# Attention and the first FFN's beginning emitted from an explicit list of pieces instead of a loop

## The chip, the cores and the metric

The kernel runs on one core of a Trainium2 chip. What counts is the device time in microseconds (us) of one execution. The kernel before took 602.12 us (median of 3 runs, 602.09 to 603.09). The execution that the profiler recorded took 603.07 us; its span, from the first to the last instruction, is 601.3 us.

## The reference

Band-and-summary attention over 2 batches, 8 heads, 768 positions and a head width of 64, and then two feed-forward networks (FFNs) over the 1536 resulting rows of 512, with 2048 inner columns each. All is float32.

```python
# attention: a query sees keys less than 16 positions away, and one summary per block of 32 keys
k_sum = k.reshape(B, H, nb, 32, D).max(axis=3)      # nb = 24 summaries
v_sum = v.reshape(B, H, nb, 32, D).mean(axis=3)
scores_l = where(|i - j| < 16, scale * q @ k.T, -1e9)
scores_s = scale * q @ k_sum.T + log(32)
a = softmax(concat([scores_l, scores_s]))            # denominator + 1e-9
x = a @ concat([v, v_sum])                           # then heads side by side: 1536 x 512
# first FFN, second FFN
h = x @ w_in;  g = h - tanh(h);              x = g @ w_out
h = x @ w_in2; g = h * tanh(log1p(exp(h)));  out = g @ w_out2
```

## The kernel before, in words

**Attention** is cut into 12 units of 128 query positions over all 8 heads (UPB = 6 units for each batch). A unit u passes through these steps, each on a fixed engine; `e` is one of two halves of the heads:

- `qk(u)`, PE: 32 score products into the PSUM tiles s (e = 0) and tr (e = 1), two buffers each (L300 to L314). It needs the queries (tile qt, three buffers), the unit's keys with their edges (tile kt, eight buffers), and the key summaries of the whole batch, which `k_sum` (DVE, one block maximum for each unit) makes and `k_fill` copies to both ends of kt. So the first unit of a batch waits for the keys of all six.
- `softmax(u, e)`: four DVE instructions add the mask and find the maximum (aa, neg), four ACT instructions take the exponential and its sum (L316 to L332).
- `norm(u)`: a reciprocal on DVE, and the multiplication of each half on POOL or DVE (L334 to L344).
- `a_trans(u, e)`: four PE transposes into the PSUM tile aT, and a copy to asb on DVE or ACT (L346 to L356).
- `av(u)`: 32 PE products with the values and value summaries (tile vu, three buffers) into the PSUM tile x (L363). The value summaries are sums by DVE or POOL (`v_sum`), a transpose, two ACT copies and four small copies within the chip (`v_trans`, `v_fill`).
- `x_hi(u)`, ACT, and `x_lo(u)`, DVE: the result as a rounded high part and the rest, the FFN's input.

**The FFNs** go over three chunks c of 512 rows, and within one over 16 steps i of 128 inner columns. A step is `ffn_in` (12 products of 128x512 on PE into s or aT), the gate (ACT tanh, DVE subtraction, ACT `g_hi`, DVE `g_lo`), and `ffn_out` (12 products, accumulated over i in x, x, tr, tr). The products are taken three times: high by high, high by low, low by high.

**The weights** come as float64 bits and are converted in 64 pieces of 256 columns for each FFN. A piece n is loaded (`conv_load`, SP), and passes `conv_top` (ACT), `conv_or` (DVE), `conv_hi` (ACT or POOL) and `conv_lo` (DVE or POOL). Six pieces can be in flight between load and `conv_or` (n_raw = 6). The first chunk's steps use each weight for the first time, so there conversion runs beside the products; later chunks use what is there.

**What sets the order.** The scheduler is off (`tc.manual_schedule`, L615): every engine carries out its instructions in the order in which the code emits them, and so does the queue of SP, which issues all DMAs and stops at one whose buffer isn't free yet. Attention's order comes from the loop over half-units j (L439 to L471): for every j it emits the scores of unit j/2, the softmax of half j-1, the normalization and the transpose of half j-5, the values of unit (j-6)/2, and what a table `todo` puts at this j (loads, block sums, fills). From j = 19 on the tables AHEAD and AFTER say how many conversion steps (`conv_tick`) go in, HI_POOL and LO_POOL whether on POOL; the first FFN's steps 0 to 5 start at fixed j through `more_in`. Then the FFN loop (L621) goes on, from n = 0, with four conversion steps for each n.

Of the kernel before, what the change touches and what calls it, by code (L numbers as in the profile page):

```python
# [26 lines left out]
def kernel(  # L27
# [17 lines left out]
    nc = tc.nc  # L45
# [125 lines left out]
    ASB_DVE = (0, 2, 7, 11, 12, 13, 14, 15, 17, 20, 21)  # L171
    NORM_DVE = (0, 13, 21, 23)
    FILL_DVE = (0, 1, 4, 5, 6, 7, 8, 9, 11)
    AHEAD = {23: 1, 24: 3, 29: 3, 31: 1}
    AFTER = {19: 1, 21: 1, 22: 1, 25: 1, 28: 3, 30: 1}
    HI_POOL = (19, 21, 22, 24, 25, 30)
    LO_POOL = (19, 22, 23, 24, 25, 28, 29, 30, 31)

    def attention(actx):
# [80 lines left out]
        def k_fill(u):  # L260
            eng = nc.vector if u in FILL_DVE else nc.gpsimd
            for o in (0, NB + KU):
                eng.tensor_copy(kt[u % NK][:, :, o:o + NB], ksum[u // UPB])

        def v_sum(b, g, part, pool=False):
            if b not in vsum:
                vsum[b] = two.tile([128, HP, NB], F32, tag="vsum", name="vsum")
            t = vtc[b, g].rearrange("p a (n c) -> p a n c", c=BLK)
            o = vsum[b][:, :, g * 8:(g + 1) * 8]
            t, o = (z[:, 2 * part:2 * part + 2] for z in (t, o))  # L270
            if not pool:
# [20 lines left out]
        def v_fill(n):  # L292
# [5 lines left out]
        sums, neg, aa, asb, xps, sc = {}, {}, {}, {}, {}, {}  # L298
# [17 lines left out]
        def softmax(u, e):  # L316
            w, pv = u % UPB, sc.pop((u, e))
            if e == 0:
                aa[u] = two.tile([128, 2, HP, KA], F32, tag="aa", name="aa", bufs=3)
                neg[u] = two.tile([128, 2, HP], F32, tag="neg", name="neg", bufs=3)  # L320
                sums[u] = two.tile([128, 2, HP], F32, tag="sums", name="sums", bufs=3)
            m = masks[0 if w == 0 else 2 if w == UPB - 1 else 1]
            for hp in range(HP):
                nc.vector.tensor_tensor_reduce(  # L324
                    out=aa[u][:, e, hp, :], in0=pv[:, hp, :], in1=m, scale=-1.0 / math.sqrt(D),
                    scalar=3.0e38, op0=ALU.add, op1=ALU.min, accum_out=neg[u][:, e, hp:hp + 1],
                )
            for hp in range(HP):
                nc.scalar.activation(  # L329
                    out=aa[u][:, e, hp, :], in_=aa[u][:, e, hp, :], func=ACTF.Exp,  # L330
                    scale=-1.0, bias=neg[u][:, e, hp:hp + 1], accum_out=sums[u][:, e, hp:hp + 1],
                )  # L332

        def norm(u):  # L334
            r = two.tile([128, 2, 2, HP], F32, tag="rd", name="rd")
# [4 lines left out]
            for e in range(2):  # L340
                (nc.vector if 2 * u + e in NORM_DVE else nc.gpsimd).tensor_tensor(
                    out=aa[u][:, e], in0=aa[u][:, e],
                    in1=r[:, 1, e, :].unsqueeze(2).to_broadcast([128, HP, KA]), op=ALU.mult,
                )  # L344
# [77 lines left out]
        at(11, L(load_vt, 1, 2), L(v_sum, 1, 0, 0))
        at(12, L(v_sum, 1, 0, 1, True), L(conv_ahead, n_raw))
        at(13, L(v_sum, 1, 1, 0))
        at(14, L(v_sum, 1, 1, 1, True))
        at(15, L(v_sum, 1, 2, 0, True))
        at(16, L(v_sum, 1, 2, 1))
        before_av[17] = L(v_trans, 1)
        at(17, L(v_fill, 1), L(v_fill, 2))
        for u in range(7, 12):  # L430
            at(2 * u - 3, L(k_fill, u))
        NJ = 2 * NU
        LT, LA = 5, 6

        def ticks(j, counts):
            for _ in range(counts.get(j, 0)):
                conv_tick(len(pieces) // 2, j in HI_POOL, j in LO_POOL)

        for j in range(NJ + LA + 2):  # L439
            if j in (NJ, NJ + 1, NJ + 5):  # L440
                more_in(n_in)
            if j == NJ:
                kq_x.close()
                more_w(4)
            xu, xr = divmod(j - LA - 2, 2)
            if xu >= 0 and not xr:
                x_hi(xu)
            if j < NJ and j % 2 == 0:
                qk(j // 2)
            nu, nr = divmod(j - 3, 2)  # L450
            nr = nr == 0 and 0 <= nu < NU
            if 1 <= j <= NJ:
                softmax(*divmod(j - 1, 2))
            ticks(j, AHEAD)
            if nr:
                norm(nu)
            if xu >= 0 and xr:
                x_lo(xu)
            if LT <= j < NJ + LT:
                a_trans(*divmod(j - LT, 2))  # L460
            if j in before_av:
                before_av[j]()
            if LA <= j < NJ + LA and (j - LA) % 2:
                av((j - LA) // 2)
# [40 lines left out]
    def gate_1(z):  # L505
        h = hs.pop(z)
        t = ts[z] = tmp.tile([128, CH], F32, tag="t", name="t")
        nc.scalar.activation(out=t, in_=h, func=ACTF.Tanh)
        nc.vector.tensor_tensor(out=t, in0=h, in1=t, op=ALU.subtract)

    def gate_1s(z):
        g_hi(z, ts[z])
        g_lo(z, ts.pop(z))
# [101 lines left out]
    with tc.manual_schedule():  # L615
        with ExitStack() as actx:
            attention(actx)
        more_w(NI - len(W))
        N2 = NC * NI
        limit = len(pieces) // 2  # L620
        for n in range(NS + 2):  # L621
# [17 lines left out]
            if f == 0:  # L639
# [14 lines left out]
                if n and n + 1 < N2:  # L654
                    gate_1(steps[n + 1])
# [102 lines left out]
```

## Time and profile before

| | |
|---|---|
| median of 3 runs | 602.12 us (602.09 to 603.09) |
| the profiled execution | 603.07 us, span 601.3 us |
| PE busy over the span | 578.8 us (96%) |
| DVE, ACT, POOL busy | 417.8, 328.5, 53.4 us |
| last unit's value products (av of unit 11) start | 82.01 us |
| bytes moved by DMA | 52.20 MB |

One execution is profiled; its instructions have a start and a duration, and an idle engine's next instruction names what released it. The profile's stretches are counted from the span's start. PE's busy time is 60.33 us in the first 79 us and has no gap behind that for hundreds of us, so the first 79 us are the stretch to look at: attention, with the first FFN's beginning in its last third.

### The profile page before, as it was taken

What the parts mean: (1) busy time and instruction counts of PE and PEld (TensorE: products, weight loads), DVE (VectorE), ACT (ScalarE), POOL (GpSimd) and SP (SyncE); (2) the same over time, 40 slices, a digit from 0 to 9 for tenths busy, and PEclk for the clock granted to TensorE, in tenths of its full rate; (3) what the DMA queues carried; (4) which work ended last, traced back from release to release, by engine and by line L of the source; (5) the groups of instructions that cost most, each with busy time, mean ns of one, the idle gap of its engine ahead of it and who ended that gap; (6) DMA issues with size and microseconds to landing.
All of it is one profiled execution on the core that took longest, in us unless ns stands there. A gap on an engine that the chain in (4) does not pass through costs nothing.

```text
span 601.3 us, 9203 instructions
## 1 busy us (share of the span) xinstructions
PE 578.8 (96%) x3212; PEld 479.0 (80%) x3212; DVE 417.8 (69%) x968; ACT 328.5 (55%) x791; POOL 53.4 (9%) x109
## 2 busy tenths in 40 slices
PE   6768899999999999999999999999999999999997
PEld 5556788888888888888888888888888888888885
DVE  5797978886251222377776489997688777597785
ACT  4788878885251122367765456664464444454442
POOL 6465660000000000000000000000000000000000
PEclk9798899999999999999999999999999999999999
DMA  9997567765020000226661102100100000100001
GB/s 271 257 306 213 154 184 238 222 218 168 0 88 0 1 0 1 62 88 192 197 186 43 40 8 63 52 2 1 55 16 1 1 1 0 71 1 1 1 1 70
DMA packets 32110, 52.20 MB, mean 87 GB/s; under 512 B 3200, under 2 KB 25728, under 8 KB 32064
## 3 DMA queue, kind: packets, MB, share of 16 engines
q1 hardware_dynamic: 32064, 51.62, 28.5%
q8 instruction: 25, 0.41, 0.3%
q14 instruction: 21, 0.17, 0.1%
HBM read 48.07 MB, written 3.15 MB: 85 GB/s over the span
## 4 chain that ended last, share of the span: by engine, by line
PE 88%; DMA 4%; DVE 3%; ACT 2%; SPq 1%; issue 1%; POOL 0%; ACTq 0%
PE aT L478 7%; PE aT L479 7%; PE tr L479 7%; PE x L479 7%; PE aT L480 7%; PE tr L480 7%; PE x L480 7%; PE x L478 7%; PE tr L478 7%; PE s L479 7%; PE s L478 7%; PE s L480 7%; DMA kt<-in_kw_dram 3%; ACT aa L329 1%; DMA vtc<-in_vt_dram 1%; PE x L363 1%
## 5 line engine op out<-in xcount | busy, mean ns | idle before, releaser
L503 DVE TENSOR_TENSOR glo<-t,ghi 128x512 fp32r<-128x512 f32 x48 | 33.4, 695 | 85.4 <-ACT ghi L498 85.4
L498 ACT ACTIVATE ghi<-t 128x512 fp32r<-128x512 f32 x48 | 30.2, 629 | 96.5 <-PE tr L480 96.5
L478 PE MATMUL aT<-xhi,w 128*128 128x512 f32 x192 | 74.9, 390 | 0.0
L478 PE MATMUL s<-xhi,w 128*128 128x512 f32 x192 | 74.9, 390 | 0.0
L480 PE MATMUL s<-xhi,w 128*128 128x512 f32 x192 | 74.7, 389 | 0.0
L480 PE MATMUL aT<-xhi,w 128*128 128x512 f32 x192 | 74.7, 389 | 0.0
L479 PE MATMUL s<-xlo,w 128*128 128x512 f32 x192 | 74.7, 389 | 0.0
L479 PE MATMUL aT<-xlo,w 128*128 128x512 f32 x192 | 74.7, 389 | 0.0
L114 ACT ACTIVATE top<-raw 128x256 f16<-128x256 bf16 x128 | 61.5, 486 | 12.2 <-ACT w L132 4.8
L121 DVE SCALAR_TENSOR_TENSOR cv<-raw,top 128x256 int32<-128x256 int32 x128 | 55.4, 434 | 11.8 <-ACT top L114 7.6
L132 ACT ACTIVATE w<-cv 128x256 fp32r<-128x256 f32 x120 | 47.6, 402 | 10.7 <-DVE cv L121 9.8
L137 DVE TENSOR_TENSOR w<-cv,w 128x256 fp32r<-128x256 f32 x114 | 48.4, 426 | 0.1
L534 DVE SCALAR_TENSOR_TENSOR t<-n,r 128x512 f32<-128x512 f32 x48 | 33.1, 689 | 17.4 <-ACT r L531 17.3
L503 DVE TENSOR_TENSOR glo<-n,ghi 128x512 fp32r<-128x512 f32 x48 | 33.1, 690 | 15.5 <-ACT ghi L498 15.5
L498 ACT ACTIVATE ghi<-n 128x512 fp32r<-128x512 f32 x48 | 30.3, 632 | 24.4 <-PE tr L479 16.1
L329 ACT ACTIVATE aa<-aa,neg 128x120 f32<-128x120 f32 x96 | 36.6, 384 | 12.4 <-DVE neg L324 12.4
L480 PEld LDWEIGHTS aT<-xhi,w 128*128 128x128 f32 x192 | 36.1, 188 | 7.5
L480 PEld LDWEIGHTS s<-xhi,w 128*128 128x128 f32 x192 | 36.1, 188 | 7.5
L478 PEld LDWEIGHTS aT<-xhi,w 128*128 128x128 f32 x192 | 36.0, 188 | 7.5
L478 PEld LDWEIGHTS s<-xhi,w 128*128 128x128 f32 x192 | 36.0, 188 | 7.5
L479 PEld LDWEIGHTS s<-xlo,w 128*128 128x128 f32 x192 | 36.0, 188 | 7.4
L479 PEld LDWEIGHTS aT<-xlo,w 128*128 128x128 f32 x192 | 36.0, 188 | 7.4
(97 smaller groups left out, 1293.1 us busy)
## 6 DMA issues: line engine op xcount, KB each, us to landing
raw<-in_w_dram SPq DMA_DIRECT2D x128, 255.8 KB, 3.6
vu<-in_vw_dram SPq DMA_DIRECT2D x24, 192.0 KB, 4.9
qt<-in_qt_dram SPq DMA_DIRECT2D x12, 256.0 KB, 4.9
vtc<-in_vt_dram SPq DMA_DIRECT2D x6, 512.0 KB, 6.7
out_dram<-o SPq DMA_DIRECT2D x9, 256.0 KB, 2.0
kt<-in_kw_dram SPq DMA_DIRECT2D x6, 320.0 KB, 8.5
kt<-in_kw_dram SPq DMA_DIRECT2D x6, 256.0 KB
out_dram<-t SPq DMA_DIRECT2D x3, 256.0 KB
```

The source lines that it names most:

```text
L114: nc.scalar.activation(out=tops[n % len(tops)].bitcast(F16).rearrange("p (n t) -> p n t", t=2)[:, :, 1], in_=raws[n].bitcast(BF16).rearran ...
L121: nc.vector.scalar_tensor_tensor(out=tmps[n], in0=raws.pop(n).bitcast(I32).rearrange("p (n t) -> p n t", t=2)[:, :, 0], scalar=13, in1=top ...
L132: nc.scalar.activation(out=hi, in_=t, func=ACTF.Copy)
L137: (nc.gpsimd if on_pool else nc.vector).tensor_tensor(out=W[i][:, 1, o:o + PW], in0=tmps.pop(n).bitcast(F32), in1=W[i][:, 0, o:o + PW].bit ...
L329: nc.scalar.activation(out=aa[u][:, e, hp, :], in_=aa[u][:, e, hp, :], func=ACTF.Exp, scale=-1.0, bias=neg[u][:, e, hp:hp + 1], accum_out= ...
L363: nc.tensor.matmul(out=xps[u][64 * e:64 * e + 64, hp, T * s:T * s + T], lhsT=vu[u % 3][:, s, 2 * hp + e, :], rhs=asb[u, e][:, hp, T * s:T ...
L478: nc.tensor.matmul(out=out, lhsT=w[0], rhs=x[0], start=first, stop=False)
L479: nc.tensor.matmul(out=out, lhsT=w[0], rhs=x[1], start=False, stop=False)
L480: nc.tensor.matmul(out=out, lhsT=w[1], rhs=x[0], start=False, stop=last)
L498: nc.scalar.activation(out=ghi, in_=t, func=ACTF.Copy)
L503: nc.vector.tensor_tensor(out=glo, in0=t, in1=ghi.bitcast(F32), op=ALU.subtract)
L534: nc.vector.scalar_tensor_tensor(out=ts[z], in0=ns[z], scalar=2.0, in1=rs[z], op0=ALU.add, op1=ALU.mult)
```

## The change

The loop over j, its tables and `todo` go. In their place stands one string of 463 names (the change's title counts 500), read from left to right; each name is a step with its unit, half or piece, and a star where a step can run on two engines. `mx` and `ex` are the two halves of what was `softmax`, `rd` and `nm` those of `norm`, `tr` and `as` the transposes and their copy, `ct`, `co`, `ch` and `cw` the four conversion steps, `in` and `ou` the FFN's products, `th`, `sb`, `gh` and `gl` the gate, and `ld...`, `cl` the loads. A star puts `kf`, `nm` and `as` on DVE, and `vs`, `ch` and `cw` on POOL. The tiles aa and neg are now one for each half instead of one for both. The list goes as far as the product `in5` and 33 pieces of conversion; the FFN loop then starts at n = 4 instead of 0.

```diff
-    ASB_DVE = (0, 2, 7, 11, 12, 13, 14, 15, 17, 20, 21)
-    NORM_DVE = (0, 13, 21, 23)
-    FILL_DVE = (0, 1, 4, 5, 6, 7, 8, 9, 11)
-    AHEAD = {23: 1, 24: 3, 29: 3, 31: 1}
-    AFTER = {19: 1, 21: 1, 22: 1, 25: 1, 28: 3, 30: 1}
-    HI_POOL = (19, 21, 22, 24, 25, 30)
-    LO_POOL = (19, 22, 23, 24, 25, 28, 29, 30, 31)
+    SEQ = """
+    ldk5 ldk4 ks5 ks4 ldk2 ks2 ldk0 ks0 ldk1 ks1 ldk3 ks3 kf4* kf2* ke4 ke3 ke1 ke2 ke5 kf0 ldq0 qk0
+    mx0.0 ex0.0 kf1 ldt0.0 mx0.1 ex0.1 vs0.0.0 vs0.0.1* kf3 ldq1 qk1 mx1.0 mx1.1 ex1.1 ex1.0 rd0
...
+    ldv11 cl14 as11.1 av11 cl15 cl16 in3 cl17 gh1 ct13 ct14 co13 co14 ch12* cw12* gl0 xh11 xl11 ct15
...
+    """.split()
...
-        def softmax(u, e):
+        def max_(u, e):
             w, pv = u % UPB, sc.pop((u, e))
-            if e == 0:
-                aa[u] = two.tile([128, 2, HP, KA], F32, tag="aa", name="aa", bufs=3)
-                neg[u] = two.tile([128, 2, HP], F32, tag="neg", name="neg", bufs=3)
-                sums[u] = two.tile([128, 2, HP], F32, tag="sums", name="sums", bufs=3)
+            aa[u, e] = two.tile([128, HP, KA], F32, tag=f"aa{e}", name="aa", bufs=3)
+            neg[u, e] = two.tile([128, HP], F32, tag=f"neg{e}", name="neg", bufs=3)
...
-        for j in range(NJ + LA + 2):
-            if j in (NJ, NJ + 1, NJ + 5):
-                more_in(n_in)
-            if j == NJ:
+        starred = ("kf", "vs", "nm", "as", "ch", "cw")
+        for z in SEQ:
+            f = z.rstrip("0123456789.*")
+            do[f](*(int(n) for n in z[len(f):].rstrip("*").split(".")), *([z[-1] == "*"] if f in starred else []))
+            if z == f"qk{NU - 1}":
                 kq_x.close()
                 more_w(4)
...
+            if z == f"av{NU - 1}":
+                actx.close()
+                more_w(NI - len(W))
...
-        for n in range(NS + 2):
+        for n in range(n_in - 2, NS + 2):
```

SP's queue, in the middle of attention's first batch: kt_95, kt_96 and kt_89 to kt_92 are the buffers that take the second batch's six key loads, vu the values, qt the queries, and a row `vu_101<-vu_100` is the copy of the value summaries. Before:

```order
L244 DMA vu_101<-in_vw_dram 96x512 x2
L240 DMA qt_97<-in_qt_dram 128x512
L244 DMA vu_102<-in_vw_dram 96x512 x2
L221 DMA kt_95<-in_kw_dram 128x4x160
L221 DMA kt_96<-in_kw_dram 128x4x160
L240 DMA qt_98<-in_qt_dram 128x512
L221 DMA kt_89<-in_kw_dram 128x4x160
L240 DMA qt_99<-in_qt_dram 128x512
L294 DMA vu_101<-vu_100 24x512 x2
L294 DMA vu_102<-vu_100 24x512 x2
L221 DMA kt_90<-in_kw_dram 128x4x160
L221 DMA kt_91<-in_kw_dram 128x4x160
```

And now:

```order
L270 DMA vtc<-in_vt_dram 128x1024
L243 DMA kt_96<-in_kw_dram 128x4x160
L243 DMA kt_89<-in_kw_dram 128x4x160
L262 DMA qt_98<-in_qt_dram 128x512
L243 DMA kt_90<-in_kw_dram 128x4x160
L266 DMA vu_100<-in_vw_dram 96x512 x2
L243 DMA kt_91<-in_kw_dram 128x4x160
L243 DMA kt_92<-in_kw_dram 128x4x160
L262 DMA qt_99<-in_qt_dram 128x512
L319 DMA vu_101<-vu_100 24x512 x2
L266 DMA vu_101<-in_vw_dram 96x512 x2
L243 DMA kt_95<-in_kw_dram 128x4x160
```

Five of the six key loads now stand ahead of the value summaries' copies, and one, kt_95, behind the first of them and a pair of value loads; before, three stood ahead and three behind.

POOL's queue, where the first conversion steps (w<-cv) stand among the normalizations (aa<-aa,rd). Before:

```order
L341 TENSOR_TENSOR aa<-aa,rd 128x480 x2
L263 COPY kt_91<-ksum 128x4x24 x2
L341 TENSOR_TENSOR aa<-aa,rd 128x480 x2
L130 CAST w_73<-cv 128x256
L341 TENSOR_TENSOR aa<-aa,rd 128x480 x2
L130 CAST w_73<-cv 128x256
```

And now:

```order
L285 COPY kt_94<-ksum 128x4x24 x2
L370 TENSOR_TENSOR aa<-aa,rd 128x480 x2
L285 COPY kt_95<-ksum 128x4x24 x2
L370 TENSOR_TENSOR aa<-aa,rd 128x480 x2
L285 COPY kt_89<-ksum 128x4x24 x2
L285 COPY kt_90<-ksum 128x4x24 x2
L370 TENSOR_TENSOR aa<-aa,rd 128x480 x2
L130 CAST w_73<-cv 128x256
```

Most fills (kt<-ksum) have come over from DVE to POOL: 9 of 12, against 3 before.

PE's queue around the last three units' value products (x<-asb), with their transposes (aT<-ident,aa) and one FFN product (aT<-xhi,w). Before:

```order
L349 MATMUL aT<-ident,aa 120x128 x4
L363 MATMUL x<-asb,vu_100 64x64 x16
L349 MATMUL aT<-ident,aa 120x128 x8
L363 MATMUL x<-asb,vu_101 64x64 x16
L349 MATMUL aT<-ident,aa 120x128 x4
L478 MATMUL aT<-xhi_67,w_75 128x512
```

And now:

```order
L378 MATMUL aT<-ident,aa 120x128 x8
L394 MATMUL x<-asb,vu_102 64x64 x16
L378 MATMUL aT<-ident,aa 120x128 x8
L394 MATMUL x<-asb,vu_100 64x64 x16
L378 MATMUL aT<-ident,aa 120x128 x8
L394 MATMUL x<-asb,vu_101 64x64 x16
L441 MATMUL aT<-xhi_67,w_75 128x512
```

The third FFN product stands between the values of units 10 and 11 in both; the first two have moved forward, to between the scores of units 9 and 10 and behind those of unit 11, and each unit's second transpose stands ahead of the value products of the unit before.

## Rows read from the trace of the kernel before

**Rows 1.** Stretches of the span: length, busy time by engine, clock, DMA share, GB/s.
```profile
core 0: us, PE busy (x) PEld busy (x) DVE busy (x) ACT busy (x) POOL busy (x), PEclk, DMA share, GB/s
0.00:82.00 82.00, 63.33 (x912) 52.25 (x912) 64.00 (x292) 61.76 (x249) 47.89 (x101) 0.90 0.81 232
11.50:82.00 70.50, 56.02 (x844) 45.33 (x844) 58.48 (x276) 58.39 (x238) 41.19 (x67) 0.88 0.80 229
97.00:145.00 48.00, 48.00 (x213) 39.75 (x213) 40.21 (x100) 38.80 (x99) 0.00 (x0) 1.00 0.71 219
```

**Rows 2.** PE in order of time, last value products: start, length, instructions.
```profile
82.01 1.15 PE L363 MATMUL x<-asb,vu 120*64 120x64 f32 x32
...
96.83 0.39 PE L478 MATMUL aT<-xhi,w 128*128 128x512 f32 x1
```

**Rows 3.** DVE's waits from 11.5 to 82 us: total, times, longest.
```profile
DVE ksum L255 <- DMA kt<-in_kw_dram: 4.9, 3, 2.9
DVE asb L353 <- PE aT L349: 2.9, 2, 1.6
DVE cv L121 <- ACT top L114: 1.3, 2, 1.1
DVE aa L324 <- PE tr L310: 1.0, 1, 1.0
```

**Rows 4.** ACT's longest wait, same stretch.
```profile
ACT aa L329 <- DVE neg L324: 12.4, 12, 2.6
```

**Rows 5.** DVE's groups up to 82 us: count, then busy us, mean ns.
```profile
L353 DVE COPY asb<-aT 120x512 f32<-120x512 f32 x11 | 7.4, 674 | 2.9 <-PE aT L349 2.9
L375 DVE TENSOR_TENSOR xlo<-x,xhi 128x512 fp32r<-128x512 f32 x10 | 6.6, 656 | 0.0
L121 DVE SCALAR_TENSOR_TENSOR cv<-raw,top 128x256 int32<-128x256 int32 x11 | 5.8, 533 | 2.2 <-ACT top L114 1.3 <-issue 0.8
L263 DVE COPY kt<-ksum 128x96 f32<-128x96 f32 x18 | 5.8, 377 | 0.1
L341 DVE TENSOR_TENSOR aa<-aa,rd 128x480 f32<-128x480 f32 x4 | 3.0, 753 | 0.1
```

**Rows 6.** ACT's groups up to 82 us.
```profile
L355 ACT ACTIVATE asb<-aT 120x512 f32<-120x512 f32 x13 | 7.5, 581 | 0.3 <-PE aT L349 0.3
L114 ACT ACTIVATE top<-raw 128x256 f16<-128x256 bf16 x12 | 5.5, 485 | 0.2 <-DVE cv L121 0.2
L132 ACT ACTIVATE w<-cv 128x256 fp32r<-128x256 f32 x4 | 1.6, 404 | 0.1
```

**Rows 7.** The chain of waits before unit 6's scores: start, length, what.
```profile
14.94 8.57 DMA kt<-in_kw_dram
...
30.19 4.37 DMA kt<-in_kw_dram
...
34.58 0.70 DVE ksum L255
```

**Rows 8.** SP's queue in order of time: the value summaries' copies, then key loads.
```profile
21.30 3.32 SPq L294 DMA_DIRECT2D vu<-vu  x4
24.84 1.76 SPq L221 DMA_DIRECT2D kt<-in_kw_dram  x2
```

**Rows 9.** PE in order of time: unit 6's first score product.
```profile
36.13 0.31 PE L310 MATMUL s<-kt,qt 64*64 64x120 f32 x1
```

**Rows 10.** POOL and DVE near 64 us, and the same DVE instruction later.
```profile
63.35 2.11 POOL L341 TENSOR_TENSOR aa<-aa,rd 128x480 f32<-128x480 f32 x2 [2.25 <-PE x L363]
...
64.54 1.20 DVE L137 TENSOR_TENSOR w<-cv,w 128x256 fp32r<-128x256 f32 x1
...
L137 DVE TENSOR_TENSOR w<-cv,w x26: 417/419/422, 90.0 to 119.9; 128x256 fp32r<-128x256 f32 x26
```

**Rows 11.** POOL's groups up to 82 us.
```profile
L341 POOL TENSOR_TENSOR aa<-aa,rd 128x480 f32<-128x480 f32 x20 | 20.8, 1055 | 22.8 <-DVE rd L339 10.1 <-ACT aa L329 6.5 <-PE x L363 5.9
L263 POOL COPY kt<-ksum 128x96 f32<-128x96 f32 x6 | 1.4, 265 | 0.0
```

More of the change, by code (lines that the diff above doesn't have):

```diff
@@ new lines @@
+    sb0 co3 ch3* co4 qk10 mx10.1 mx10.0 ex9.0 rd9 cl5 ct5 ldq11 cl6 cl7 vf1.1 av6 xh6 xl6 tr8.0
+    ex10.1 ex10.0 kf11 qk11 ct6 co5 mx11.1 ct7 ex11.1 as8.0* cw3* in1 ldv7 av7 xh7 nm9.0* tr9.0
+    as9.0 as8.1* rd10 nm9.1* mx11.0 ch4* cw4* xl7 tr9.1 as9.1* co6 co7 ex11.0 rd11 vf1.2 ldv8 av8
+    xh8 xl8 nm10.0 nm10.1 tr10.1 as10.1 ch5* tr10.0 as10.0* cl8 ct8 co8 gh0 ch6 ldv9 av9 cw5* cw6
+    ch7* ch8 cw7 cw8 xh9 xl9 cl9 ct9 co9 cl10 ldv10 ct10 co10 nm11.0 tr11.0 as11.0 th1 sb1 nm11.1
+    tr11.1 av10 in2 xh10 xl10 cl11 ct11 co11 cl12 cl13 ct12 co12 ch9* ch10* cw9 ch11* cw10 cw11
@@ new lines @@
+    ldv11 cl14 as11.1 av11 cl15 cl16 in3 cl17 gh1 ct13 ct14 co13 co14 ch12* cw12* gl0 xh11 xl11 ct15
+    ct16 cl18 cl19 cl20 ch13* cw13 ch14 gl1 co15 ct17 ch15 co16 cw14 cw15 ch16* cw16* cl21 cl22 co17
+    cl23 ch17 ct18 ct19 co18 cl24 ct20 ch18* co19 cl25 ct21 th2 cw17 co20 cw18* co21 ch19* cw19 ct22
+    sb2 co22 ct23 co23 cl26 cl27 cl28 ch20 ch21* cw20 cw21* ct24 th3 ct25 ch22 cw22 co24 ct26 co25
+    ct27 cl29 cl30 ou0 ou1 ch23 ch24 cw23 co26 co27 ct28 gh2 ct29 sb3 gl2 ch25 ch26 co28 cw24* co29
@@ L179, in attention @@
+    cw25 ct30 co30 cl31 cl32 ct31 cw26 co31 ch27 cw27* ch28* ch29* cw28 cw29* ct32 ch30* cw30* cl33
+    cl34 cl35 cl36 cl37 in4 th4 ch31 sb4 gh3 gl3 in5
+    """.split()
     def attention(actx):
@@ L339, in norm, with a_out @@
             nc.vector.reciprocal(out=r[:, 1], in_=r[:, 0])
[L340 to L344, printed above, removed]
+        def norm(u, e, star):
+            r = sums[u, 1]
+            (nc.vector if star else nc.gpsimd).tensor_tensor(
+                out=aa[u, e], in0=aa[u, e],
+                in1=r[:, 1, e, :].unsqueeze(2).to_broadcast([128, HP, KA]), op=ALU.mult,
+            )
         def a_trans(u, e):
-            p = pst("aT")
+            p = at[u, e] = pst("aT")
             for hp in range(HP):
-                nc.tensor.transpose(p[0:KA, hp * 128:(hp + 1) * 128], aa[u][:, e, hp, :], ident)
+                nc.tensor.transpose(p[0:KA, hp * 128:(hp + 1) * 128], aa[u, e][:, hp, :], ident)
+        def a_out(u, e, star):
             t = two.tile([KA, HP, 128], F32, tag=f"asb{e}", name="asb")
-            pv = p[0:KA, :].rearrange("p (a n) -> p a n", a=HP)
-            if 2 * u + e in ASB_DVE:
+            pv = at.pop((u, e))[0:KA, :].rearrange("p (a n) -> p a n", a=HP)
+            if star:
                 nc.vector.tensor_copy(t, pv)
@@ L422, in attention @@
[L422 to L437, printed above, removed]
@@ L439, in attention @@
-        for j in range(NJ + LA + 2):
-            if j in (NJ, NJ + 1, NJ + 5):
-                more_in(n_in)
-            if j == NJ:
+        do = dict(
+            ldk=lambda u: (load_k_own if u < UPB else load_k)(u), ldq=load_q, ldv=load_v, ldt=load_vt,
+            ks=k_sum, ke=k_edges, kf=k_fill, vs=v_sum, vt=v_trans, vE=v_out, vf=v_fill,
+            qk=qk, mx=max_, ex=exps, rd=recip, nm=norm, tr=a_trans, av=av, xh=x_hi, xl=x_lo,
+            cl=conv_load, ct=conv_top, co=conv_or, ch=conv_hi, cw=conv_lo,
+            th=lambda i: gate_1t(steps[i]), sb=lambda i: gate_1m(steps[i]),
+            gh=lambda i: g_hi(steps[i], ts[steps[i]]), gl=lambda i: g_lo(steps[i], ts.pop(steps[i])),
+            ou=more_out,
+        )
@@ L443, in attention @@
+        do["as"] = a_out
+        do["in"] = more_in
+        starred = ("kf", "vs", "nm", "as", "ch", "cw")
[3 more added lines that the diff above has]
+            if z == f"qk{NU - 1}":
                 kq_x.close()
                 more_w(4)
[L445 to L464, printed above, removed]
@@ L503, in g_lo, with gate_1t, gate_1m @@
         nc.vector.tensor_tensor(out=glo, in0=t, in1=ghi.bitcast(F32), op=ALU.subtract)
-    def gate_1(z):
-        h = hs.pop(z)
+    def gate_1t(z):
         t = ts[z] = tmp.tile([128, CH], F32, tag="t", name="t")
[L508 to L513, printed above, removed]
+        nc.scalar.activation(out=t, in_=hs[z], func=ACTF.Tanh)
+    def gate_1m(z):
+        nc.vector.tensor_tensor(out=ts[z], in0=hs.pop(z), in1=ts[z], op=ALU.subtract)
     def gate_2u(z):
@@ L615 @@
     with tc.manual_schedule():
-        with ExitStack() as actx:
+        actx = ExitStack()
+        with actx:
             attention(actx)
-        more_w(NI - len(W))
+        n0, n1, n2, n3, nl = (sum(z[:2] == f for z in SEQ) for f in ("ct", "co", "ch", "cw", "cl"))
         N2 = NC * NI
         limit = len(pieces) // 2
-        for n in range(NS + 2):
+        for n in range(n_in - 2, NS + 2):
             z = f, c, i = steps[n] if n < NS else (2, 0, n - NS)
@@ L654 @@
                 if n and n + 1 < N2:
-                    gate_1(steps[n + 1])
+                    gate_1t(steps[n + 1])
+                    gate_1m(steps[n + 1])
                 if n == N2 - 2:
```

85 lines of the change are left out of this document (29 added, 56 removed).

## The prediction

> **What bounds the kernel now.** I read the busy times by stretch first, then PE in order of time, then the waits of each engine, and last the groups of instructions of the stretch in which PE waits.
>
> From 97 to 145 us PE is busy 48.00 of 48 us at full clock [rows 1], and the page's row of busy tenths shows 9 for PE from there to the last slices: there the time is PE's work, which the change leaves alone. Up to 82 us PE is busy 63.33 us, DVE 64.00, ACT 61.76, POOL 47.89, and the DMA share is 0.81 [rows 1]: no engine is full, so order decides. At 82.01 us the value products of the last unit (av of unit 11) start; from their end, 83.16, to 96.83 PE carries out five FFN products of 2.73 us each without a gap [rows 2]. The new list has the same five behind the same point (in3, ou0, ou1, in4, in5), and three FFN products ahead of it, as before. So a microsecond by which av of unit 11 starts earlier is a microsecond off the whole time, as long as PE doesn't wait behind it. The question is where that start goes.
>
> In the stretch from 11.5 us (the first exponentials) to 82 us, DVE is idle 70.5 - 58.48 = 12.0 us and ACT 70.5 - 58.39 = 12.1 us [rows 1]. ACT waits for DVE's maxima almost alone [rows 4]; DVE waits 4.9 us for key loads, 2.9 us for transposes, 1.3 us for the conversion's first step, 1.0 us for scores [rows 3].
>
> **The change part by part.** First the work on each engine ahead of av of unit 11, by counting the list's names up to `av11` against the groups up to 82 us.
>
> DVE: 15 copies of transposed weights instead of 11 (+4 x 0.674 = +2.7 us), 3 fills instead of 9, two copies each (-12 x 0.377 = -4.5), 2 normalizations instead of 4 (-2 x 0.753 = -1.5), 11 `xlo` instead of 10 (+0.7), 13 `cv` instead of 11 (+2 x 0.533 = +1.1), all from [rows 5]; 6 conversion rests instead of 1, which I price like a `cv` of the same shape (+5 x 0.533 = +2.7). Sum +1.2: 59.7 us from 11.5 us on, so without any idle time DVE is there at 71.2 us.
>
> ACT: 9 copies instead of 13 (-4 x 0.581 = -2.3), 13 `top` instead of 12 (+0.5), 2 high parts instead of 4 (-0.8) [rows 6], and one gate rounding more, which I price like the copy (+0.6). Sum -2.0: 56.4 us, so ACT is there at 67.9 us at the earliest. For ACT this bound is strict, since the last copy (`as11.1`) is its own; DVE has conversion steps in it that may come late.
>
> POOL: 22 normalizations instead of 20 (+2 x 1.055) and 18 fill copies instead of 6 (+12 x 0.265) [rows 11]; its conversion steps stay 16. 41.19 + 5.3 = 46.5 us, far from full. PE's 56.02 us are the same work.
>
> Second, the waits. The key loads: now the last of the second batch's six stands behind the first two of the four summary copies; before, it was issued at 30.19 us, landed 4.37 us later, and unit 6's scores came at 36.13 us [rows 7, 9]. The four copies took from 21.30 to 24.62 us on SP, and the next key load went out at 24.84 [rows 8]. So the last load goes out between 21.30 + 3.32 / 2 = 23.0 and 24.8 us, lands 4.37 to 8.57 us later (the two landings in the chain of waits) [rows 7], and with 0.70 us for the block maxima and 2 x 0.265 us for the fill on POOL unit 6's scores come between 28.6 and 34.6 us: 1.5 to 7.5 us earlier. The 4.9 us that DVE waits for keys should go, and with deeper run-ahead the 1.0 us for scores too: 5.9 of its 12.0 us. What hides the loads is the work on three units' scores already made; if that cover fails, the wait is back on the same instruction.
>
> The other 6.1 us (transposes, conversion, small gaps) I leave as they are; the list orders them anew, and no row shows how. DVE: 71.2 + 6.1 = 77.3 us. ACT waits for DVE's maxima, so the same 5.9 us go from its 12.1: 67.9 + 6.2 = 74.1 us. I take 76.0, nearer to DVE, since ACT follows it. That is 6.0 us before 82.0.
>
> The two ends: with no idle time left on DVE 71.2 us (10.8 us gained), with all of the old 12.0 us on its longer work 83.2 us (1.2 us lost).
>
> Third, behind it. `ou0` now stands ahead of `in4`: it needs the first gate's rest and both x tiles from unit 11, 2.73 us after the value products instead of 5.46. Two DVE steps and one on ACT stand there (0.6 to 0.7 us each by [rows 5, 6]), so I cost it at nothing; if DVE trails by more than 1 to 2 us, PE waits that much. In the following stretch DVE is busy 40.21 and ACT 38.80 of 48 us [rows 1]: the conversion moves forward with PE and has 8 us of room in 48.
>
> DMA: 19 MB in 82 us (232 GB/s, share 0.81) [rows 1] become nearly as much in 76, a share of about 0.87. I cost it at nothing; its price is in the landing times above.
>
> The sum: 603.07 - 6.0 = 597.1 us against the profiled execution. That one was 0.95 us slower than the median of 602.12, so a median run should take 596.1 us.
>
> **A row and a rule on POOL and DVE.** Near 64 us, while POOL carries out two normalizations, a DVE subtraction of two SBUF tiles takes 1.20 us; the same instruction takes 0.417 later, when POOL is idle [rows 10]. Over the 11 `cv` the mean is 0.533, so 0.12 us above that free value [rows 5]; the sum above has 19 such instructions (13 and 6) with 19 x 0.12 = 2.2 us of it. The Trainium skill (SBUF — State Buffer, Who interferes with whom) says that a VectorE instruction with two SBUF inputs, or in a two-port mode, and a GpSimd instruction that reads SBUF exclude each other for a whole instruction; the trace agrees in this place. It speaks against the change, which loads POOL more in a shorter stretch. As a mechanism, from rows: POOL is busy 46.5 of 64.5 us, 0.72; an instruction that meets it waits half a normalization, 0.53 us; 19 x 0.72 x 0.53 = 7.2 us instead of 2.2. By that, av of unit 11 starts at 81.0 us, and the time is 601.1. The mean of 0.533, measured with POOL busy 41.19 of 70.5 us, contradicts so high a price, and I keep the rows' value.
>
> **Rivals.**
>
> *The list packs nearly full.* The gaps between transposes, copies and conversion close too, and DVE idles 1 us instead of 4.8: start at 72.2, gain 9.8, 592.3 us. For it: three engines have 12 us of idle time each with no single owner. Against it: in-order queues, with DVE and ACT both needed at 0.9 of the stretch. Chance 0.16.
>
> *The waits only change place.* The last key load lands late (34.6 us), or the norm on POOL holds the transposes, and 10 to 12 us of idle time stay: start at 81 to 83 us, 601 to 603 us. For it: POOL gets 5.3 us more in a chain from exponential to transpose, and five queues must fit together. Against it: unit 6's scores come earlier even in the bad case. Chance 0.16.
>
> *POOL and DVE block each other: slower.* If each of the 19 instructions waits as the one at 64.54 us, 0.78 us, they cost 14.8 us instead of 2.2, and the end moves to 88.6. It decides from 0.43 us for each (19 x (0.43 - 0.12) = 6 us); at 0.6, the middle of 0.43 and 0.78, the cost is 9.1 us more than in the sum and the time 605.2 us. For it: the row at 64.54. Against it: the mean over 11. Chance 0.11.
>
> **How the numbers follow.** Forecast, 594 to 599.5 us, 0.57; nearly full, 0.16; waits moved, 0.16; slower, 0.11. About 0.2% (1.2 us) can be told from no change here. Faster by more: 0.57 + 0.16 + 0.06 of the moved waits = 0.79; within: 0.10; slower: 0.11. The range goes from 590.5, just past the earliest start by DVE (602.1 - 10.8 = 591.3), to 601.5, which takes in the better half of the moved waits and leaves out 0.16 above and 0.03 below.
>
> **What would show it.** Right: DVE's wait for key loads behind 11.5 us falls from 4.9 us to under 1.5, unit 6's scores come before 35 us, av of unit 11 starts between 73 and 79 us, PE shows no wait behind it, and ACT's wait for maxima is about half of 12.4 us. The means of `cv` and of the subtraction on DVE stay under 0.6 us. Wrong: PE waits for x or the first gate's rest behind av of unit 11; or `cv` over 0.8 us; or the wait for keys moves to unit 6's load and stays 5 us; or PE gaps appear between 100 and 150 us, because conversion no longer keeps up with a PE that started earlier.

## The result, and the profile after

The changed kernel takes 595.34 us in the median of 4 runs (594.36 to 597.15); the kernel before takes 602.15 beside it (4 runs, 602.09 to 603.09). The ratio is 0.9887, with a 95% interval of 0.9861 to 0.9913. The forecast was 596.1 us. The profiled execution of after took 597.15 us, 1.8 us more than the median, with a span of 595.2 us against 601.3 before.

The first view of after is the busy time by stretch, with the columns of [rows 1]. The third line ends 0.4 us behind the start of unit 11's value products.

```profile
core 0: us, PE busy (x) PEld busy (x) DVE busy (x) ACT busy (x) POOL busy (x), PEclk, DMA share, GB/s
0.00:82.00 82.00, 64.68 (x968) 53.44 (x969) 68.82 (x301) 62.94 (x255) 52.68 (x120) 0.96 0.88 255
11.50:82.00 70.50, 58.22 (x920) 47.19 (x913) 63.89 (x291) 60.10 (x244) 45.42 (x82) 0.95 0.89 254
11.50:75.60 64.10, 51.84 (x868) 41.81 (x860) 58.29 (x280) 57.04 (x236) 43.55 (x79) 0.95 0.92 259
97.00:145.00 48.00, 48.00 (x214) 39.74 (x213) 36.18 (x86) 33.54 (x83) 2.35 (x3) 1.00 0.59 189
```

DVE and ACT do in 64.1 us what took 70.5 [rows 1]: 58.29 and 57.04 us of work, so 5.8 and 7.1 us of idle time instead of 12.0 and 12.1. The mean granted clock of PE is 0.95 instead of 0.88. On nearly the same work PE is busy 51.84 us instead of 56.02 and idle 12.3 instead of 14.5: two thirds of what PE saves goes with the higher clock, one third with shorter waits (E9 and E10 below ask what the clock is worth). What PE waits for has changed too (11.5 to 82 us: total, times, longest), first before and then after:

```profile
PE x L363 <- ACT asb L355: 4.7, 4, 2.2
PE x L363 <- DVE asb L353: 3.1, 2, 1.6
...
PE aT L378 <- POOL aa L370: 4.1, 4, 2.5
PE x L394 <- DMA vu<-in_vw_dram: 3.6, 6, 1.0
```

The 7.8 us for copies of transposed weights are gone; in the new list each unit's second transpose stands ahead of the value products of the unit before. What PE waits for now are divisions on POOL and value loads. PE in order of time shows where the gain arrives:

```profile
75.20 1.45 PE L394 MATMUL x<-asb,vu 120*64 120x64 f32 x32 [0.86 <-DVE w L137]
...
90.33 0.39 PE L441 MATMUL aT<-xhi,w 128*128 128x512 f32 x1
```

The last value products start at 75.20 instead of 82.01 us and the sixth FFN product behind them at 90.33 instead of 96.83 [rows 2]. From their end to the end of the span it is 518.55 us (518.14 before), with PE busy 514.62 (514.31 before): the gain is complete at this point. The waits of DVE and then of ACT, 11.5 to 82 us (total, times, longest), answer to [rows 3, 4]:

```profile
DVE aa L347 <- PE tr L335: 3.1, 3, 1.6
DVE cv L121 <- ACT top L114: 1.1, 2, 0.7
DVE ksum L277 <- DMA kt<-in_kw_dram: 0.7, 1, 0.7
...
ACT aa L356 <- DVE neg L347: 2.9, 2, 1.9
ACT w L132 <- DVE cv L121: 2.0, 2, 1.4
ACT top L114 <- DMA raw<-in_w_dram: 1.9, 2, 1.1
```

Of DVE's waits, the one for key loads is down from 4.9 to 0.7 us, the one for transposes (2.9) is gone, and the one for scores has grown from 1.0 to 3.1. ACT's wait for maxima fell from 12.4 to 2.9 us; its waits for `cv` and for raw weights are new, but most of the one (1.4 us) and half of the other (1.0) lie behind the start of unit 11's value products. SP's queue and unit 6's first scores answer to [rows 8, 9]:

```profile
17.61 4.11 SPq L243 DMA_DIRECT2D kt<-in_kw_dram  x2
...
22.94 1.80 SPq L319 DMA_DIRECT2D vu<-vu  x2
...
25.80 0.62 SPq L243 DMA_DIRECT2D kt<-in_kw_dram  x1
```
```profile
32.52 0.28 PE L335 MATMUL s<-kt,qt 64*64 64x120 f32 x1 [0.63 <-POOL kt L285]
```

Two key loads go out at 17.61 us and the last at 25.80, behind one pair of summary copies; it lands 5.4 us later, and the scores come at 32.52 us instead of 36.13.

### The profile page after: what moved, and what is told of

Same layout as the page of the kernel before. It is cut to its first block, busy times and chain, and to the rows that moved or that the text cites. A ratio compares the mean times of both kernels' runs of the same rounds, so it can differ in the third digit from the quotient of the medians.

```text
span 595.2 us, 9226 instructions
## 1 busy us (share of the span) xinstructions
PE 573.9 (96%) x3212; PEld 474.6 (80%) x3212; DVE 416.9 (70%) x958; ACT 322.2 (54%) x776; POOL 61.6 (10%) x134
## 4 chain that ended last, share of the span: by engine, by line
PE 85%; DMA 6%; DVE 4%; ACT 1%; issue 1%; SPq 1%; POOL 0%; DVEq 0%; ACTq 0%; POOLq 0%
PE x L442 7%; PE tr L442 7%; PE x L443 7%; PE tr L441 7%; PE tr L443 7%; PE x L441 7%; PE aT L442 7%; PE aT L441 7%; PE aT L443 7%; PE s L442 7%; PE s L441 7%; PE s L443 7%; DMA raw<-in_w_dram 3%; DMA vu<-in_vw_dram 1%; DVE cv L121 1%; DVE aa L347 1%
## 5 line engine op out<-in xcount | busy, mean ns | idle before, releaser
L121 DVE SCALAR_TENSOR_TENSOR cv<-raw,top 128x256 int32<-128x256 int32 x128 | 57.5, 456 | 9.9 <-ACT top L114 7.3
L132 ACT ACTIVATE w<-cv 128x256 fp32r<-128x256 f32 x109 | 42.8, 400 | 10.1 <-DVE cv L121 9.6
L479 ACT ACTIVATE t<-aT 128x512 f32<-128x512 f32 x24 | 14.4, 598 | 44.3 <-PE aT L443 30.8
```

The costliest lines, as they stand in the source:

```text
L121: nc.vector.scalar_tensor_tensor(out=tmps[n], in0=raws.pop(n).bitcast(I32).rearrange("p (n t) -> p n t", t=2)[:, :, 0], scalar=13, in1=top ...
L132: nc.scalar.activation(out=hi, in_=t, func=ACTF.Copy)
L479: nc.scalar.activation(out=t, in_=hs[z], func=ACTF.Exp)
```

## The experiments

Each was timed beside the kernel before on the same chip. One table first, since a single time explains almost all of it: the start of the last single value product of unit 11, and how much of the span is left then. The clock is PE's mean granted clock from 11.5 to 82 us. These times are those of one profiled execution, the ratio is that of the medians: E3's profiled execution took 3.1 us more than its median, E2's 1.6 us less.

| kernel | last value product, us | span, us | difference | clock | ratio to before, 95% |
|---|---|---|---|---|---|
| before | 82.9 | 601.3 | 518.4 | 0.88 | 1 |
| after (profiled with the result) | 76.4 | 595.2 | 518.8 | 0.95 | 0.9887 (0.9861 to 0.9913) |
| after again (E0) | 73.9 | 592.5 | 518.6 | 0.98 | 0.9879 (0.9859 to 0.9900) |
| E1 keys late | 81.1 | 599.8 | 518.7 | 0.91 | 0.9962 (0.9949 to 0.9976) |
| E2 products behind | 74.6 | 603.3 | 528.7 | 0.88 | 1.0066 (1.0043 to 1.0089) |
| E3 fills of before | 85.7 | 605.3 | 519.6 | 0.84 | 1.0008 (0.9992 to 1.0023) |
| E4 no conversion on POOL | 81.4 | 600.7 | 519.3 | 0.90 | 0.9995 (0.9980 to 1.0010) |
| E5 old order, new engines | 85.0 | 603.3 | 518.3 | 0.85 | 1.0052 (1.0032 to 1.0072) |
| E6 new order, old engines | 97.8 | 616.2 | 518.4 | 0.83 | 1.0231 (1.0199 to 1.0263) |
| E7 four value buffers | 79.3 | 598.7 | 519.4 | 0.90 | 0.9952 (0.9936 to 0.9968) |
| E8 old order, keys early | 83.0 | 601.3 | 518.3 | 0.85 | 1.0023 (1.0007 to 1.0039) |
| E9 after, clock filled | 74.9 | 593.9 | 519.0 | 1.00 | 0.9896 (0.9871 to 0.9921) |
| E10 before, clock filled | 84.5 | 602.9 | 518.4 | 0.90 | 1.0014 (1.0000 to 1.0028) |
| E11 copies, divisions of before | 87.6 | 606.1 | 518.5 | 0.83 | 1.0061 (1.0043 to 1.0079) |

Except in E2, which moves products across the point, 518.3 to 519.6 us are left in every kernel. So each experiment is a question about one time: when PE gets to unit 11's values.

**Is it the loads? (E1, E8)** The theory was that earlier key loads and the run-ahead they allow give the gain; the rival, that the new choice of engines does.

```diff
 E1, list of after
-... ldt0.2 ldk7 ldk8 ldq4 ldk9 ... mx3.0 ks7 ks9 ldv0 ldk10 ldk11 ldq5 ... vf0.1 nm1.1 ... ks10
+... ldt0.2 ldq4 ... mx3.0 ldv0 ldq5 ... vf0.1 ldk7 ldk8 ldk9 ldk10 ldk11 nm1.1 ... ks7 ks9 ks10
 E8, places of before
+at(1, L(load_k, 6), L(load_k, 7))
+at(2, L(load_k, 8))
-at(5, L(v_fill, 1), L(v_fill, 2), L(load_k, 9), L(load_k, 10))
+at(5, L(load_k, 10), L(v_fill, 1), L(v_fill, 2))
...
```

> The changed kernel with one part undone: five of the second batch's six key loads go behind the first copies of the value summaries, where the sixth already stands, and the first two block maxima behind them. Theory of order (the gain comes from waits that the new order removes): the last key load goes out near 29 us, unit 6's scores start at 35 to 39 us instead of 32.5, DVE waits 3 to 7 us for keys, and the time is 598 to 601.5 us. Theory of engines (the gain comes from work taken off DVE): the wait is hidden by scores made ahead, and the time stays under 596.5 us.

> The kernel before with one part of the change alone: the second batch's key loads are emitted as early as their buffers allow, ahead of value loads and of the copies of the value summaries; all else as it was. Theory of order, key loads as its largest part: DVE's wait for keys behind 11.5 us falls from 4.9 to under 1.5 us, unit 6's scores come 3 to 5 us earlier than 36.1, and the time is 598 to 600.5 us. If the wait only moves (values late, or transposes), 601 to 603 us.

E1 took 600.98 us beside 603.26 for the kernel before: with the keys late, the new list keeps 0.4% of its 1.1%. Waits of DVE, then PE, from 11.5 to 82 us in E1:

```profile
DVE ksum L276 <- DMA kt<-in_kw_dram: 5.8, 4, 2.4
...
PE x L393 <- DMA vu<-in_vw_dram: 10.2, 9, 7.1
```

The wait for keys is back, and the value loads, now behind the keys in SP's queue, hold PE for 10.2 us (3.6 in after); unit 6's scores come at 38.56 us. So E1's loss is that of late keys and late values together. E8 is the other half: the same kind of loads early, in the old order. It took 604.82 us beside 603.26, no gain and a small loss. Its waits, PE and then DVE, and then the chain of work that ended last, where unit 3's scores start:

```profile
PE s L310 <- DMA qt<-in_qt_dram: 8.1, 3, 4.9
...
DVE aa L324 <- PE aT L349: 5.5, 1, 5.5
```
```profile
15.08 10.11 DMA qt<-in_qt_dram
25.19 0.04 issue
25.23 0.46 PE s L310
```

DVE's wait for keys in this stretch is gone, and in its place PE waits 4.9 us, up to 25.23, for unit 3's queries (before, these scores start at 20.41 us). That load now goes out behind three key loads, at 15.08 us instead of 12.34, and by the chain takes 10.11 us to land; whether the key loads beside it stretch the landing was not tried. Unit 6's scores, for which the keys were moved, come at 38.69 us, later than before's 36.13. So the early loads are needed in the new list, and early keys by themselves are worth nothing in the old one: the next load in the queue is then the late one. My expectation for E8 fell; its rival came nearer.

**Is it the engines? (E5, E6, E3, E11)** The old order with the new choice of engines, the new order with the old choice, and the two parts of the old choice alone.

```diff
 E5, numbers of before replaced by those in after's list
-ASB_DVE = (0, 2, 7, 11, 12, 13, 14, 15, 17, 20, 21)
+ASB_DVE = (0, 1, 3, 4, 6, 8, 9, 10, 11, 13, 15, 16, 17, 19, 20)
-NORM_DVE = (0, 13, 21, 23)
+NORM_DVE = (18, 19)
-FILL_DVE = (0, 1, 4, 5, 6, 7, 8, 9, 11)
+FILL_DVE = (2, 4, 7)
 E6: the stars of after's as, nm and kf pieces set by before's numbers
 E3: kf only       E11: as and nm only
-... kf6 qk6 ... kf8 kf9 ...
+... kf6* qk6 ... kf8* kf9* ...
```

> The kernel before, in its old order, with the new choice of engines for attention: the copies of transposed weights 15 instead of 11 on DVE, the normalizations 2 instead of 4, the fills 3 instead of 9. Theory of engines: 597 to 599 us, most of the gain. Theory of order: 600.5 to 603 us, since DVE's and ACT's waits of 12 us each stay.

> The changed kernel's list with the choice of engines of the kernel before (eight more fills on VectorE and one fewer, fourteen of the asb copies and six of the divisions on another engine). If the order alone brings the gain: within 1 us of the changed kernel, span 594 to 596.5. If order and choice belong together (the choice alone, on the old order, had cost about 3 us): between, span 597 to 600, with VectorE over 66 us busy from 11.5 to 82 us or new waits of TensorE for aa. If the choice of engines were what brings the gain in this order: 601.

> The changed kernel with the kernel before's choice for the key fills alone: units 0, 1, 5, 6, 8, 9 and 11 on VectorE, unit 2 on GpSimd. With all choices of the kernel before the list had taken 616 us. If the fills are what did it (a fill in VectorE's queue stands behind conversions, and the scores of its unit wait for it): TensorE waits 6 us or more for kt from VectorE from 11.5 to 90 us, and the kernel takes 608 to 618. If the asb copies and divisions did it: 596 to 599, for 12 more copies of some 0.26 us on VectorE.

> The changed kernel with the kernel before's choice for the asb copies and divisions alone, the fills as in the changed kernel. If the fills made the 616 us: 596 to 600. If the copies and divisions made it (a transposed unit waits for an asb copy behind eight exponentials on ScalarE): 606 to 614, with ScalarE's wait of xhi for TensorE above 10 us.

Measured: E5 606.41 us beside 603.26; E6 616.41 beside 603.15; E3 604.01 and E11 606.90, both beside 603.23. Neither half works alone: old order with new engines 0.5% slower, new order with old engines 2.3% slower, both together 1.1% faster. In E5, too, DVE has no wait for keys left from 11.5 to 82 us, with the loads untouched: it waits 7.4 us for transposes and 5.6 for scores. E6 went past everything I had expected of it; E3 and E11 show why. DVE and then PE in order of time in E3, then PE's longest wait in E11 (11.5 to 82 us):

```profile
32.86 0.69 DVE L276 TENSOR_REDUCE ksum<-kt 128x16 f32<-128x512 f32 x1 [2.04 <-DMA kt<-in_kw_dram]
33.58 0.57 DVE L284 COPY kt<-ksum 128x96 f32<-128x96 f32 x4
34.08 0.46 PE L334 MATMUL s<-kt,qt 64*64 64x120 f32 x1 [5.91 <-DVE kt L284]
```
```profile
PE aT L377 <- DVE aa L369: 7.8, 3, 3.4
```

These are unit 5's scores, and the list loads unit 5's own keys first of all. But the fill of unit 5, two copies of 0.2 us each, now stands in DVE's queue behind the block maximum of unit 6's keys, and DVE waits 2.04 us for that load: PE waits 5.91 us, and the scores start at 34.08 us instead of 28.69. In after this fill is POOL's and doesn't stand behind the load. In E11 PE's longest wait is for divisions on DVE; the copies were moved along with them, and the two were not tried apart. The 616 us were no single cause: against after, E3 loses 1.3 points, E11 1.8, and both together 3.5. I had set E3 at 608 to 618 or 596 to 599; it came between. E11 fell into its second range (606 to 614), without the sign that I had given for it: ACT waits 7.9 us for value products, not over 10.

**Are POOL and DVE in each other's way? (E4)**

```diff
-... co0 ch0* kf10 cw0* ... ch1* ... cw1* in0 ... ch2* nm8.0 cw2* ...
+... co0 ch0 kf10 cw0 ... ch1 ... cw1 in0 ... ch2 nm8.0 cw2 ...
```

> The changed kernel with the thirteen splitting steps (ch) and eight subtractions or so (cw) that GpSimd does ahead of unit 11's products with the values given to ScalarE and VectorE. Work theory (VectorE and ScalarE nearly full up to there): some 13 x 0.43 us = 5.6 us more on ScalarE and 8 x 0.5 = 4 us more on VectorE, unit 11 at 77 to 80 us, span 597 to 600. Lock theory (GpSimd's big operations stretch the copies and conversions on VectorE): cv's mean falls from 0.56 to below 0.50 us, copies shorter, VectorE gains more than it takes on, span 593 to 595.

E4 took 602.61 us beside 603.15, some 6.5 us more than after on the same chip (596.08). The list has ten `ch` and six `cw` on POOL ahead of unit 11's values, not the thirteen and eight of my expectation. DVE's groups from 11.5 to 82 us, and PE's longest wait there:

```profile
L121 DVE SCALAR_TENSOR_TENSOR cv<-raw,top 128x256 int32<-128x256 int32 x14 | 6.7, 500 | 0.5 <-ACT top L114 0.5
L137 DVE TENSOR_TENSOR w<-cv,w 128x256 fp32r<-128x256 f32 x12 | 5.4, 481 | 6.1 <-ACT w L132 6.1
```
```profile
PE s L442 <- DVE w L137: 5.0, 2, 3.5
```

With POOL busy 36.33 instead of 45.42 us, `cv` on DVE does get shorter (0.500 instead of 0.563), in the lock theory's direction though not below its 0.50, and the copies `asb` stay at 0.677. POOL's share is worth far more than that: DVE then waits 6.1 us for ACT's high parts, and PE 5.0 us for converted weights in the first FFN products. The work theory holds, and the loss is larger than I had put it.

**What are the products between the units worth? (E2)**

```diff
-... in0 th0 ... sb0 ... in1 ... gh0 ... th1 sb1 ... in2 ... av11 cl15 cl16 in3 cl17 gh1 ...
+... av11 in0 th0 sb0 gh0 in1 th1 sb1 gh1 in2 cl15 cl16 in3 cl17 ...
```

> The changed kernel with the first three FFN products (in0, in1, in2) and their gates moved behind the last unit's value products. If they cost nothing where they stand (PE has 12 us of idle time up to there), 8.2 us of PE work come behind, less what the last value products gain by starting earlier (0 to 3.5 us, since in2 stands straight ahead of them): 600 to 603.5 us. If the products hold up transposes and scores where they stand, most comes back: 595 to 598 us.

E2 took 607.02 us beside 603.26, more than I had expected. Taking the three products of 2.73 us out from between the units brings the last value product only from 76.4 to 74.6 us, and 8.2 us of products are then still to do. The rest is the clock; PE in order of time in E2:

```profile
71.54 0.48 PE L393 MATMUL x<-asb,vu 120*64 120x64 f32 x4 [2.33 <-DMA vu<-in_vw_dram]
73.11 1.76 PE L393 MATMUL x<-asb,vu 120*64 120x64 f32 x28 [1.09 <-DMA vu<-in_vw_dram]
74.80 0.80 PE L440 MATMUL s<-xhi,w 128*128 128x512 f32 x1
75.40 0.63 PE L441 MATMUL s<-xlo,w 128*128 128x512 f32 x1
...
78.08 0.40 PE L442 MATMUL s<-xhi,w 128*128 128x512 f32 x1
```

The granted clock from 74.80 to 80.00 us is 0.72 on average: behind waits of 2.33 and 1.09 us the first products run at 1.2 GHz, 0.43 us from start to start instead of 0.23. That is 0.28 x 5.2 = 1.5 us. With 8.2 it makes 9.7 of the 9.9 us by which E2's difference in the table exceeds after's. The kernel before also has three products between its units, so their standing there is no part of the gain. That two of them stand earlier now was not tried, nor what before would lose without them.

**Is it the clock? (E9, E10)** The clock rises with the gain in the table. Products of the identity matrix that change no result fill PE's waits.

```diff
 E9, after
-    NWARM = 18
+    NWARM = 32
+            if (u, e) == (0, 1):
+                for _ in range(8):
+                    nc.tensor.matmul(out=p[:, 0:128], lhsT=ident, rhs=ident, start=True, stop=True)
 E10, before, ahead of each unit's value products
+            for _ in range(3):
+                nc.tensor.matmul(out=px[:, 0:128], lhsT=ident, rhs=ident, start=True, stop=True)
```

> The changed kernel with 14 more warm-up products of the identity matrix at the start (18 before, 3.4 us more, into a wait of 3.7 us for the first keys) and eight of them (1.9 us) ahead of the first transposes, into a wait of 2.5 us. The clock was at 0.5 from about 11 to 14.5 us and again from 18 to 21 us. Theory A: both stretches go to 1.0, the scores and transposes there come 1 to 2 us earlier and the span is 592 to 594. Theory B: the clock rises and the span stays within 0.7 us of 592.5 to 595.2, as the conversions set the pace. Theory C: 596 or more.

> The kernel before with three products of the identity matrix ahead of each unit's products with the values, written into the same tile and overwritten there: no result changes. They fall into the places where TensorE waited longest (for asb, 0.8 to 2.2 us) and cost 12 x 3 x 0.24 = 8.6 us of TensorE's time. Theory A, the low clock after such waits is a cost of its own: the mean granted clock from 11.5 to 82 us rises from 0.88 to 0.93 or more and the span falls from 601.3 to 598 to 600.5. Theory B, the run-up is paced by VectorE and ScalarE, and the clock only follows the waits: the clock rises and the span stays within 0.7 us of 601.3. Theory C, the products delay what is behind them: span 602 to 607.

E9 took 595.99 us beside 603.23. Its busy times by stretch, same columns as above:

```profile
11.50:82.00 70.50, 58.99 (x938) 47.50 (x931) 64.74 (x293) 61.05 (x247) 46.16 (x83) 1.00 0.90 259
```

The clock is 1.00 in the whole run-up and the ratio, 0.9896, lies inside the interval of after (E0: 0.9859 to 0.9900). A span of 593.9 us fits the ranges of both my first cases, so the ratio has to decide: in after the missing clock costs nothing that can be measured, to within some 1.5 us (0.25%). At least a part of what the clock gives stands there as waiting: PE waits 5.7 us for value loads instead of 3.6. E10 raised the clock of before only from 0.88 to 0.90, less than expected, and took 604.12 us beside 603.23. It shows no gain, but it doesn't settle what the low clock costs in before: how much of the change's gain runs through the clock stays open.

**Can the waits left in after be taken away? (E7, with E0)**

```diff
-vu = [con.tile([KA, 2, H, D], F32, name=f"vu{n}") for n in range(3)]
+vu = [con.tile([KA, 2, H, D], F32, name=f"vu{n}") for n in range(4)]
-... vE0 vf0.1 ... ldv1 ldk6 ... vf0.2 ... ldv2 cl0 ldv3 av2 ...
+... vE0 ldk6 vf0.1 ... ldv1 ... vf0.2 vf0.3 ... ldv2 ldv3 cl0 ldv4 av2 ...
```

> The changed kernel as it is, again, so that the three others are held against it on one chip. Both theories: ratio to the kernel before 0.9887, within 0.986 to 0.992; TensorE reaches unit 11's products with the values near 75 us and its mean granted clock from 11.5 to 82 us is near 0.95.

> The changed kernel with four buffers for the values instead of three, each load of them from unit 3 on one place earlier in the list, and the last key load ahead of the summary copies. If TensorE's waits for values (3.6 us from 11.5 to 82 us) and VectorE's last wait for keys (0.7 us) stand on the path: those two waits under 0.8 us together, unit 11 at 73 to 74.5 us, span 592.5 to 594.5. If the conversions on VectorE and ScalarE set the pace: the waits go and the span stays at 594.5 to 596, since the products behind the units then wait for converted weights.

E0 took 596.08 and E7 600.06 us beside 603.15: cutting the named waits down cost 4 us. SP's queue and PE in E7:

```profile
26.03 3.86 SPq L318 DMA_DIRECT2D vu<-vu  x4
29.93 1.93 SPq L265 DMA_DIRECT2D vu<-in_vw_dram  x4
```
```profile
59.06 0.34 PE L393 MATMUL x<-asb,vu 120*64 120x64 f32 x4 [1.69 <-DMA vu<-vu]
```

PE's wait for values fell from 3.6 to 1.1 us and DVE's for the last keys from 0.7 to 0.3. But the fourth buffer needs its own pair of summary copies in SP's queue (3.86 us in one piece), PE waits 2.2 us for such copies elsewhere, and ACT waits 6.8 us for value products (1.5 in after). Neither of my two cases came true. Which of the edits (the fourth buffer, the earlier value loads, the earlier key load) costs most was not tried. No experiment beat the changed kernel.

## Why the prediction was right, point by point

- **All of it is decided at unit 11's values.** Right: after them 518.55 us are left, 518.14 before. The start was forecast at 76.0 us and measured at 75.20 us in the profile and at 72.48 in E0's. The median gained 6.8 us against 6.0 in the forecast.
- **Work on the engines.** DVE 59.7 us forecast, 58.29 measured; ACT 56.4 and 57.04. POOL 46.5 and 43.55.
- **Idle time.** DVE 4.8 us in the forecast (76.0 - 71.2), 5.8 measured; ACT 8.1 and 7.1. The sum held, its parts did not: of the 5.9 us that I let go, the keys gave 4.2, and the wait for scores, which I took away, grew by 2.1. The 2.9 us for transposes, which I left, went instead. That the errors of this step cancelled is luck. Nor are the parts fixed: in E0, the same program in an execution of 594.59 us, DVE is idle only 2.4 us up to 72.48 us, close to the start of 72.2 of the rival *nearly full*, and its waits for keys and scores (11.5 to 82 us) are

```profile
DVE ksum L277 <- DMA kt<-in_kw_dram: 1.1, 1, 1.1
DVE aa L347 <- PE tr L335: 1.0, 1, 1.0
```

- **What the loads are worth.** The prediction read DVE's 4.9 us for keys as time to be had. As a statement on this list it held (E1, where values come late as well). As a price of that wait alone it is wrong: in the old order it buys nothing (E8). The step "5.9 us of waits go, so the end comes 6 us earlier" needed the rest of the list, above all fills, divisions and copies whose engine no longer holds up what PE waits for (E3, E11), and I had costed the change of engines only as work, +1.2 us on DVE.
- **Unit 6's scores** at 32.52 us, in the range of 28.6 to 34.6. The last key load went out at 25.80 us, 1.0 us behind the latest time that I had given, and its landing of 5.4 us, near the short end of 4.37 to 8.57, made up for it.
- **ACT's wait for maxima** is 2.9 us, not the half of 12.4 that I gave as a sign; up to 75.2 us ACT also waits 1.5 us for value products, 0.9 for raw weights and 0.6 for `cv`.
- **`ou0` at nothing.** Right: PE shows no wait behind unit 11 in the list of waits.
- **DMA share** 0.91 from 0 to 75.6 us, a little more than 0.87; ACT waits 0.9 us for raw weights and PE 3.6 us for value loads, and what of that the share costs was not tried apart.
- **POOL against DVE.** `cv` takes 0.563 us on average, with POOL busy 0.68 of the stretch (43.55 of 64.1): dearer than 0.533, under the sign of 0.6, and short of the 0.43 us above the free value that the rival needed. The mean of the nine subtractions is 0.497 (0.608 for ten in E0). The Trainium skill's rule (SBUF — State Buffer, Who interferes with whom) agrees in direction: E4, with less work on POOL, has 0.500 and 0.481. The high price that I had worked out beside it, 0.53 us for each meeting, is not what the trace shows: up to 75.2 us 13 `cv` of 0.576 us and 6 subtractions of 0.535 cost 2.8 us over the free 0.417, against 2.2 in the sum and 7.2 by that price. Groups of DVE up to 82 us in after, with those of [rows 5] and the subtraction:

```profile
L384 DVE COPY asb<-aT 120x512 f32<-120x512 f32 x15 | 10.0, 677 | 0.0
L121 DVE SCALAR_TENSOR_TENSOR cv<-raw,top 128x256 int32<-128x256 int32 x18 | 9.8, 563 | 1.1 <-ACT top L114 1.1
L406 DVE TENSOR_TENSOR xlo<-x,xhi 128x512 fp32r<-128x512 f32 x12 | 8.1, 674 | 0.9 <-ACT xhi L402 0.7
...
L137 DVE TENSOR_TENSOR w<-cv,w 128x256 fp32r<-128x256 f32 x9 | 4.2, 497 | 0.2 <-ACT w L132 0.2
```

- **The chances.** Slower (0.11) and the part of the moved waits above 601.5 us (0.08 for a half) leave 0.19 above the range, not 0.16; nothing rests on it.

What stays open: which of the list's many moves carry the gain. The experiments show that the early loads, POOL's fills, the new engines for divisions and copies (together) and POOL's conversion are each needed in it, and that early keys or the new engines alone are worth nothing; they don't divide the 6.8 us among them. The move of the transposes ahead of the value products, with which PE's 7.8 us of waits for copies went, has no experiment of its own.

## What to carry to other kernels

Where five in-order queues feed one another, look for the one instruction behind which all the time is fixed, and hold every variant against its start: here what is left behind it agrees within 1.3 us in thirteen of fourteen profiles. A wait in such a stretch is not the price of what it waits for: taken away alone it turned up on the next load (E8) or copy (E7). A copy of 0.2 us in the wrong queue held PE for 5.91 us (E3), so the order and the choice of engines are searched together.

## What the hardware showed unexpectedly

- FFN products behind waits of 2.33 and 1.09 us ran at 1.2 GHz at first (E2: 0.43 us a step instead of 0.23), while a full clock in the run-up of after brought nothing that could be measured (E9). Behind unit 11's values PE works without a gap, and there a low clock is time lost; ahead of them, in after, it was not.
- The same program's run-up varies: after's last value product came at 76.4 us in one profile and at 73.9 in another, with the rest equal to 0.2 us.
